# The order of SyncE's closing waits in a one-core SiLU MLP kernel, forward and backward

## Chip, cores and metric

The kernel runs on 1 core of one Trainium2 chip. The metric is device time in microseconds (us). A run is one execution; where several are given, the text says how many. The span in a profile goes from the first to the last instruction of the program; the device time is longer than the span by 1.8 us in most runs. Where the text below says what "the clock" tells, it means this measured device time; TensorE's own clock is named as such.

The change is a small one: its subject is the last microsecond of 320.

## The reference

```python
# x: [1, 2048, 640], w1: [640, 1536], w2: [1536, 640], grad_out: [1, 2048, 640], all bf16
h = jnp.einsum("bsd,df->bsf", x, w1)
h = jax.nn.silu(h)
out = jnp.einsum("bsf,fd->bsd", h, w2)
# returned: out and the gradients of x, w1 and w2 for grad_out (by jax.vjp)
```

## The kernel before

About 310 us of the kernel are one unbroken row of matmuls on TensorE. The head: 22 warm-up matmuls on a constant tile, then 20 transposes of the first rows of x, then the first real group.

```python
NWARM = 22
...
early = [nc.vector.memset(warm[:], 1.0)]
...
for i in range(NWARM):
    early.append(nc.tensor.matmul(wp[:, 0:P], lhsT=warm[:], rhs=warm[:], start=True, stop=True))
ident = cpool.tile([P, P], dt_in, name="ident")
make_identity(nc, ident[:])
...
early += [load_x_half(0), load_x_half(1), load_w1_rows(0, 1), load_w1_rows(1, KM)]
...
nc.tensor.transpose(tp[:, q, :], x_two[:, half, q, dt_ * P:(dt_ + 1) * P], ident[:])
```

The tail: the last tile of the gradient of w1 is computed in two parts, of 384 and 128 columns, and each part is stored as soon as it is evicted.

```python
for k, (lo, hi) in enumerate(((0, FC - P), (FC - P, FC))):
    ...                                     # 16 matmuls into gp[:, lo:hi]
    if k == 0:
        nc.scalar.activation(g1[:, lo:hi], gp[:, lo:hi], ACT.Copy)
    else:
        nc.vector.tensor_copy(out=g1[:, lo:hi], in_=gp[:, lo:hi])
    nc.sync.dma_start(out=gw1_v[:, dt_, fc * FC + lo:fc * FC + hi], in_=g1[:, lo:hi])
continue
```

The kernel's source has nothing after that. The framework adds a closing block: SyncE waits until eleven semaphores of DMAs and engines have their final values, then all engines meet in a barrier, the semaphores are cleared, and they meet once more. In the compiled program of before, SyncE's part of it reads as follows (a number is a semaphore: 101 and 104 to 110 count DMAs, 99, 100 and 102 count instructions of GpSimd, VectorE and ScalarE, TensorE's 103 is not waited for, 96 and 97 belong to the barrier; 101 is that of the 96 KB store, 104 that of the last one, of 32 KB):

```
EventSemaphore  wait 106, 105
EventSemaphore  wait 107, 104      <- the last store
EventSemaphore  wait 108, 101
EventSemaphore  wait 109, 100
EventSemaphore  wait 110, 102
Drain           wait 99
Drain           wait 97 == 0, then add 1 to 96     <- "reporting drain": SyncE is here
```

GpSimd waits until 96 has four such reports, and then releases the engines (in the trace of before its wait on 96 starts at 318.250 us, 33 ns after SyncE's reporting drain, and its update of 97 at 318.328). In the source this is one drain with a list of eleven waits, 99 first; in this program the compiler left the first of the list on the drain and put the others, two by two, into instructions ahead of it: five pairs and the drain in the trace.

Of the kernel before, what the change touches and what calls it, by code (L numbers as in the profile page):

```python
# [1 line left out]

# [12 lines left out]
def start_before_entry_wait(nc, names):  # L15




    def move(nc):  # L20
        blocks = nc.m.functions[0].blocks
        entry, home = blocks[0].instructions, blocks[1].instructions
        for engine in {i.engine for i in home if i.name in names}:
            mine = [i for i in home if i.engine == engine]
            last = max(k for k, i in enumerate(mine) if i.name in names)
            moved = mine[: last + 1]
            gate = next(
                k
                for k, i in enumerate(entry)
                if i.engine == engine and isinstance(i, mybir.InstEventSemaphore)  # L30
            )
            taken = {i.name for i in moved}
            for k in reversed(range(len(home))):
                if home[k].name in taken:
                    del home[k]
            for i in reversed(moved):
                entry.insert(gate, i)

    nc.at_finalize(move)

# [2 lines left out]
def kernel(  # L43
# [11 lines left out]
    nc = tc.nc  # L55
# [43 lines left out]
    def store_rows(c, pool):  # L99
        for scr, dst_v in ((oT_scr, out_v), (gxT_scr, gx_v)):  # L100
            o_sb = pool.tile([P, STC, D], dt_in, name="o_sb")
            nc.sync.dma_start_transpose(out=o_sb[:], in_=scr[:, c * SC:(c + 1) * SC])
            nc.sync.dma_start(out=dst_v[:, c * STC:(c + 1) * STC, :], in_=o_sb[:])
# [3 lines left out]
    def load_a_blk(fc, pool, tag=None):  # L107
        a_blk = pool.tile([P, ST, FC], dt_in, name="a_blk", tag=tag or "a_blk")
        nc.sync.dma_start_transpose(out=a_blk[:], in_=aT_scr[fc * FC:(fc + 1) * FC, :])
        a_blks.append(a_blk)  # L110

    with ExitStack() as mctx:
# [47 lines left out]
        early += [load_x_half(0), load_x_half(1), load_w1_rows(0, 1), load_w1_rows(1, KM)]  # L160
        load_w1_rows(KM, DT)
        start_before_entry_wait(nc, {i.ins.name for i in early})
        for fc in range(1, NFC):
            load_w1(fc * FC, (fc + 1) * FC)
# [147 lines left out]
    with ExitStack() as fctx:  # L312
        ab2pool = fctx.enter_context(tc.tile_pool(name="ab2pool", bufs=NFC - 1))
        gbpool = fctx.enter_context(tc.tile_pool(name="gbpool", bufs=NFC))
        fpool = fctx.enter_context(tc.tile_pool(name="fpool", bufs=NFC))
        s1pool = fctx.enter_context(tc.tile_pool(name="s1pool", bufs=3))

        for fc in range(1, NFC):
            load_a_blk(fc, ab2pool)
        gh_blks = []  # L320
        for fc in range(NFC):
            gh_blk = gbpool.tile([P, ST, FC], dt_in, name="gh_blk")
            nc.sync.dma_start_transpose(out=gh_blk[:], in_=ghT_scr[fc * FC:(fc + 1) * FC, :])
            gh_blks.append(gh_blk)

        store_rows(NCH - 1, s1pool)

        gw2_v = gw2.rearrange("(ft p) d -> p ft d", p=P)
        g2T_v = g2T_scr[:].rearrange("(dt p) f -> p dt f", p=P)
        k = 0  # L330
        for fc in range(NFC):
            a_blk = a_blks[fc]
            g2T = fpool.tile([P, DT, FC], dt_in, name="g2T")
            for dt_ in range(DT):
                gp = ps_h.tile([P, FC], FP32, name="hp")
                for st in range(ST):
                    nc.tensor.matmul(  # L337
                        gp[:],
                        lhsT=go_nat[:, st, dt_ * P:(dt_ + 1) * P],
                        rhs=a_blk[:, st, :],  # L340
                        start=(st == 0),
                        stop=(st == ST - 1),
                    )
                if k % 2 == 0:
                    nc.scalar.activation(g2T[:, dt_, :], gp[:], ACT.Copy)  # L345
                else:
                    nc.vector.tensor_copy(out=g2T[:, dt_, :], in_=gp[:])  # L347
                k += 1
            nc.sync.dma_start(out=g2T_v[:, :, fc * FC:(fc + 1) * FC], in_=g2T[:])

        def store_gw2(fc):
            g2 = fpool.tile([P, FB, D], dt_in, name="g2")
            nc.sync.dma_start_transpose(out=g2[:], in_=g2T_scr[:, fc * FC:(fc + 1) * FC])
            nc.sync.dma_start(out=gw2_v[:, fc * FB:(fc + 1) * FB, :], in_=g2[:])

        gw1_v = gw1.rearrange("(dt p) f -> p dt f", p=P)
        k = 0
        for fc in range(NFC):
            gh_blk = gh_blks[fc]
            for dt_ in range(DT):  # L360
                if dt_ == DT // 2:
                    store_gw2(fc)
                if fc == NFC - 1 and dt_ == DT - 1:
                    for k, (lo, hi) in enumerate(((0, FC - P), (FC - P, FC))):
                        gp = ps_h.tile([P, FC], FP32, name="hp")
                        for st in range(ST):
                            nc.tensor.matmul(  # L367
                                gp[:, lo:hi],
                                lhsT=x_nat[:, st, dt_ * P:(dt_ + 1) * P],
                                rhs=gh_blk[:, st, lo:hi],  # L370
                                start=(st == 0),
                                stop=(st == ST - 1),
                            )
                        g1 = s1pool.tile([P, FC], dt_in, name="g1")
                        if k == 0:
                            nc.scalar.activation(g1[:, lo:hi], gp[:, lo:hi], ACT.Copy)
                        else:
                            nc.vector.tensor_copy(out=g1[:, lo:hi], in_=gp[:, lo:hi])  # L378
                        nc.sync.dma_start(
                            out=gw1_v[:, dt_, fc * FC + lo:fc * FC + hi], in_=g1[:, lo:hi]  # L380
                        )
                    continue
                gp = ps_h.tile([P, FC], FP32, name="hp")
                for st in range(ST):
                    nc.tensor.matmul(  # L385
                        gp[:],
                        lhsT=x_nat[:, st, dt_ * P:(dt_ + 1) * P],
                        rhs=gh_blk[:, st, :],
                        start=(st == 0),
                        stop=(st == ST - 1),  # L390
                    )
                g1 = s1pool.tile([P, FC], dt_in, name="g1")
                if k % 2 == 0:
                    nc.scalar.activation(g1[:], gp[:], ACT.Copy)
                else:
                    nc.vector.tensor_copy(out=g1[:], in_=gp[:])  # L396
                k += 1
                nc.sync.dma_start(out=gw1_v[:, dt_, fc * FC:(fc + 1) * FC], in_=g1[:])
# [30 lines left out]
```

## Time and profile before

| | before |
|---|---|
| device time, median of the first 3 runs | 321.83 us (321.44 to 322.0) |
| device time of the profiled run | 320.68 us |
| span of the profiled run | 318.9 us |
| TensorE busy | 315.2 us, 99% |
| last matmul group's eviction starts | 316.10 us |
| last store (32 KB): issue, landing | 316.42 us, 317.90 us |
| SyncE's reporting drain starts | 318.217 us |
| landing of the last store to end of span | 1.011 us |

These are lines of the page of before: the span, the busy times of the engines, and the chain of work that ended last. In all such lines PE is TensorE with its matmuls, PEld its weight loads, DVE VectorE, ACT ScalarE, POOL GpSimd, SPq the queue of SyncE, and L424 line 424 of the kernel.

```profile
span 318.9 us, 3570 instructions
...
PE 315.2 (99%) x1498; PEld 145.4 (46%) x1498; DVE 102.2 (32%) x182; ACT 77.7 (24%) x142; POOL 0.7 (0%) x6
...
PE 98%; DMA 1%; DVE 1%; issue 0%; DVEq 0%; SPq 0%
```

TensorE is the whole chain, but for 1 to 2%. So what SyncE does in the middle holds up nothing that the chain shows; what it does when TensorE has finished should count fully, because then nobody else works. The next two lines are the DMA view of the stretch from 315 to 320 us of before: the two last stores, with size and microseconds from issue to landing.

```profile
out_dram<-g SPq DMA_DIRECT2D x1, 96.0 KB, 1.6
out_dram<-g SPq DMA_DIRECT2D x1, 32.0 KB, 1.5
```

The next line is from the view of waits of SyncE's queue (microseconds in total, times, longest), and the two after it are the instructions of the closing block on SyncE from 316.7 to 318.3 us (duration in ns: shortest, median, longest; then when the first and the last of them start).

```profile
SPq L424 <- DMA out_dram<-g: 1.1, 1, 1.1
```

```profile
L424 SPq EVENT_SEMAPHORE  x5: 28/28/1051, 316.8 to 318.1; - x5
L424 SPq DRAIN  x2: 7/10/13, 318.1 to 318.2; - x2
```

One of the five pairs of waits lasts 1.05 us, the other four 28 ns each. The trace has each of them as a record, so their starts can be listed (us from the span's start; this list is made from the records):

```
wait 106, 105        316.798   28 ns
wait 107, 104        316.867 1051 ns   ends 317.918; the last store landed at 317.896
wait 108, 101        317.957   28 ns
wait 109, 100        318.022   28 ns
wait 110, 102        318.083   28 ns
drain, wait 99       318.148   13 ns
reporting drain      318.217    7 ns
```

A wait that is met already still takes 61 to 69 ns from its start to the start of the next instruction. Four instructions stand between the wait that matters and the reporting drain.

### The profile page before, as it was taken

How to read it: one execution, taken by the hardware profiler on the slowest of the kernel's cores; microseconds unless marked ns; L12 is line 12 of the kernel's file. 1: busy time of each engine (PE TensorE's matmuls, PEld its weight loads, DVE VectorE, ACT ScalarE, POOL GpSimd, SP SyncE). 2: the span in 40 equal slices, each digit the busy share in tenths (PEclk: the TensorE clock that was granted, in tenths of full speed). 3: DMA queues.
4: the chain of work that ended last, by engine and by line, in shares of the span. 5: the costliest groups of instructions: out<-in, count | busy, mean ns of one | idle time of the engine just before them, and what ended most of it. 6: DMA issues, size and time to landing. Idle time of an engine off the chain costs nothing.

```text
span 318.9 us, 3570 instructions
## 1 busy us (share of the span) xinstructions
PE 315.2 (99%) x1498; PEld 145.4 (46%) x1498; DVE 102.2 (32%) x182; ACT 77.7 (24%) x142; POOL 0.7 (0%) x6
## 2 busy tenths in 40 slices
PE   9999999999999999999999999999999999999996
PEld 6444444444444444444444444444444444444443
DVE  2871641477410187700157741000001100001001
ACT  4951000644201354311065410111000001001100
POOL 0000000000000000000000000000000000000000
DMA  8999999998999866382643089719999998995011
GB/s 274 319 173 221 250 243 277 334 289 264 290 288 305 199 200 166 109 286 82 166 128 119 2 279 264 200 45 285 272 207 270 262 249 288 239 293 194 34 48 34
DMA packets 147311, 67.33 MB, mean 211 GB/s; under 512 B 112608, under 2 KB 147040, under 8 KB 147296
## 3 DMA queue, kind: packets, MB, share of 16 engines
q1 hardware_dynamic: 147296, 67.12, 81.5%
q8 instruction: 11, 0.18, 0.2%
q14 instruction: 4, 0.03, 0.0%
HBM read 9.83 MB, written 28.97 MB: 122 GB/s over the span
## 4 chain that ended last, share of the span: by engine, by line
PE 98%; DMA 1%; DVE 1%; issue 0%; DVEq 0%; SPq 0%
PE hp L249 32%; PE hp L186 16%; PE hp L337 16%; PE hp L233 16%; PE hp L385 15%; PE hp L367 1%; DMA x_two<-in_x_dram 1%; DVE xT L179 0%; PE tp L177 0%; DVE g L378 0%; DVEq L378 0%; SPq L413 0%
## 5 line engine op out<-in xcount | busy, mean ns | idle before, releaser
L186 PE MATMUL hp<-xT,w_nat 128*128 128x512 bf16 x240 | 56.9, 379 | 0.2 <-DVE xT L179 0.2
L233 PE MATMUL hp<-goT,w2T 128*128 128x512 bf16 x240 | 56.9, 379 | 0.0
L249 PE MATMUL hp<-aT,w_nat 128*128 128x512 bf16 x240 | 52.5, 379 | 0.0
L249 PE MATMUL hp<-ghT,w1T 128*128 128x512 bf16 x240 | 52.5, 379 | 0.0
L337 PE MATMUL hp<-a_blk,go_nat 128*128 128x512 bf16 x240 | 52.0, 379 | 0.0
L385 PE MATMUL hp<-gh_blk,x_nat 128*128 128x512 bf16 x224 | 48.5, 379 | 0.0
L257 ACT ACTIVATE oT<-hp 128x512 bf16<-128x512 f32 x24 | 14.3, 597 | 109.8 <-PE hp L249 109.8
L195 ACT ACTIVATE aT<-hp 128x512 bf16<-128x512 f32 x48 | 29.9, 625 | 32.8 <-PE hp L186 32.8
L186 PEld LDWEIGHTS <-w_nat 128*128 128x128 bf16 x240 | 23.5, 98 | 28.4 <-issue 0.4
L233 PEld LDWEIGHTS <-w2T 128*128 128x128 bf16 x240 | 23.5, 98 | 28.3
L337 PEld LDWEIGHTS <-go_nat 128*128 128x128 bf16 x240 | 23.5, 98 | 28.3
L249 PEld LDWEIGHTS <-w1T 128*128 128x128 bf16 x240 | 23.5, 98 | 28.3
L249 PEld LDWEIGHTS <-w_nat 128*128 128x128 bf16 x240 | 23.4, 98 | 28.3
L259 DVE CAST oT<-hp 128x512 bf16<-128x512 f32 x16 | 11.1, 692 | 77.0 <-PE hp L249 77.0
L240 DVE SCALAR_TENSOR_TENSOR ghT<-ghT,hp 128x512 bf16<-128x512 bf16 x48 | 32.5, 681 | 7.3 <-PE hp L233 7.3
L385 PEld LDWEIGHTS <-x_nat 128*128 128x128 bf16 x224 | 21.9, 98 | 26.4
L202 DVE SCALAR_TENSOR_TENSOR ghT<-aT,v 128x512 bf16<-128x512 bf16 x48 | 32.7, 686 | 0.5
L201 DVE TENSOR_SCALAR v<-t 128x512 bf16<-128x512 f32 x48 | 20.2, 425 | 30.1 <-ACT t L199 30.1
L199 ACT ACTIVATE t<-hp 128x512 f32<-128x512 f32 x48 | 29.8, 625 | 0.0
L396 DVE CAST g<-hp 128x512 bf16<-128x512 f32 x7 | 4.8, 691 | 47.1 <-PE hp L385 27.6
L347 DVE CAST g2T<-hp 128x512 bf16<-128x512 f32 x7 | 4.8, 692 | 46.1 <-PE hp L337 46.1
L345 ACT ACTIVATE g2T<-hp 128x512 bf16<-128x512 f32 x8 | 4.8, 597 | 47.0 <-PE hp L337 47.0
(20 smaller groups left out, 25.2 us busy)
## 6 DMA issues: line engine op xcount, KB each, us to landing
aT_scr<-aT SPq DMA_DIRECT2D x4, 1536.0 KB, 7.1
ghT_scr<-ghT SPq DMA_DIRECT2D x4, 1536.0 KB, 8.0
out_dram<-o_sb SPq DMA_DIRECT2D x8, 640.0 KB, 3.6
oT_scr<-oT SPq DMA_DIRECT2D x4, 640.0 KB, 3.6
go_nat<-in_grad_out_dram SPq DMA_DIRECT2D x4, 640.0 KB, 6.6
x_nat<-in_x_dram SPq DMA_DIRECT2D x4, 640.0 KB, 5.4
gxT_scr<-oT SPq DMA_DIRECT2D x4, 640.0 KB, 4.7
w_nat<-in_w_dram SPq DMA_DIRECT2D x1, 1920.0 KB, 13.7
```

Source lines behind the costliest of these rows:

```text
L186: nc.tensor.matmul(hp[:], lhsT=w1_nat[:, dt_, ft * P:(ft + 1) * P], rhs=xT[:, dt_, :], start=(dt_ == 0), stop=(dt_ == DT - 1),)
L195: nc.scalar.activation(aT[:, ft, :], hp[:], ACT.Silu)
L199: nc.scalar.activation(t[:], hp[:], ACT.Tanh, scale=0.5)
L201: nc.vector.tensor_scalar(out=v[:], in0=t[:], scalar1=-0.5, scalar2=0.5, op0=ALU.mult, op1=ALU.add)
L202: nc.vector.scalar_tensor_tensor(out=ghT[:, ft, :], in0=aT[:, ft, :], scalar=1.0, in1=v[:], op0=ALU.subtract, op1=ALU.mult)
L233: nc.tensor.matmul(gp[:], lhsT=w2T[:, dt_, ft * P:(ft + 1) * P], rhs=goT[:, dt_, :], start=(dt_ == 0), stop=(dt_ == DT - 1),)
L240: nc.vector.scalar_tensor_tensor(out=ghT[:, ft, :], in0=ghT[:, ft, :], scalar=1.0, in1=gp[:], op0=ALU.add, op1=ALU.mult)
L249: nc.tensor.matmul(op_[:], lhsT=w_all[:, ft, dt_ * P:(dt_ + 1) * P], rhs=rhs_all[:, ft, :], start=(ft == 0), stop=(ft == FT - 1),)
L257: nc.scalar.activation(oT[:, dt_, :], op_[:], ACT.Copy)
L259: nc.vector.tensor_copy(out=oT[:, dt_, :], in_=op_[:])
L337: nc.tensor.matmul(gp[:], lhsT=go_nat[:, st, dt_ * P:(dt_ + 1) * P], rhs=a_blk[:, st, :], start=(st == 0), stop=(st == ST - 1),)
L385: nc.tensor.matmul(gp[:], lhsT=x_nat[:, st, dt_ * P:(dt_ + 1) * P], rhs=gh_blk[:, st, :], start=(st == 0), stop=(st == ST - 1),)
```

## The change

The intent: all waits that are met early go ahead, and run while the last store is in flight; the wait for the last store comes last of all. A hook that runs when the program is complete puts its entry at the front of the list, since in before the first of the list is the one that stayed on the drain.

```diff
+import copy
...
+def wait_for_last_store_last(nc, name):
+    def move(nc):
+        blocks = nc.m.functions[0].blocks
+        store = next(i for b in blocks for i in b.instructions if i.name == name)
+        lanes = {u.id for u in store.sync_info.on_update}
+        end = blocks[-1].instructions
+        at = next(k for k, i in enumerate(end) if i.engine == mybir.EngineType.SP)
+        waits = list(end[at].sync_info.on_wait)
+        late = [w for w in waits if w.id in lanes]
+        assert len(late) == 1 and not end[at].sync_info.on_update
+        waits = late + [w for w in waits if w.id not in lanes]
+        end[at] = copy.replace(end[at], sync_info=mybir.SyncInfo(on_wait=waits, on_update=[]))
+
+    nc.at_finalize(move)
...
-                        nc.sync.dma_start(
+                        last_store = nc.sync.dma_start(
                             out=gw1_v[:, dt_, fc * FC + lo:fc * FC + hi], in_=g1[:, lo:hi]
                         )
+                    wait_for_last_store_last(nc, last_store.ins.name)
                     continue
```

## The prediction

> **What bounds the kernel.** The page gives PE 315.2 us busy of a 318.9 us span (99%), and the chain that ended last is 98% PE. The change touches none of that, only the tail. In the trace the last two stores (96 KB and 32 KB, line 379) are issued at 315.67 and 316.42 us; the 32 KB one lands at 317.90, 1.48 us after its issue. [...]1.48 us for 32 KB agrees with a latency, and the change doesn't shorten it.
>
> After the issue SyncE runs its closing sequence (line 424): five instructions that each wait for two semaphores, a drain with the eleventh wait, then the drain that reports to the closing barrier. The second pair holds the last store's semaphore: it starts at 316.87 and lasts 1.05 us (the view of waits: "SPq L424 <- DMA out_dram<-g: 1.1"), to 317.918, 22 ns after the landing. The others take 28 ns each, but behind the long one come three pairs and the drain, 61 to 66 ns from start to start: 317.957, 318.022, 318.083, drain 318.148 to 318.161, reporting drain 318.217. So 299 ns pass from the end of the long wait to the reporting drain, for semaphores that had their values long before.
>
> **What the change does.** The same eleven waits; the last store's moves to the front of the list. In the program of before, the first entry of that list (GpSimd's semaphore) stayed on the drain and the rest went into pairs ahead of it. So I expect the last store's wait alone on the drain, after the other ten in five pairs. Nothing is added or removed. [...]
>
> **Cost.** The five pairs then run while the last store is in flight. The latest semaphore among them is the 96 KB store's, landed at 317.29, in the second pair; three more pairs follow, so the drain starts to wait near 317.54, some 350 ns early. It ends about 22 ns after the landing, 317.92; the reporting drain follows 56 ns later, as it does now behind the drain: 317.975 instead of 318.217. Saving 299 - 56 = 243 ns, all on the critical path: the other engines' drains ended by 316.45, and GpSimd waits for four reports, of which SyncE's is last. The two barrier rounds behind it (0.68 us) are unchanged.
>
> Predicted: span 318.9 to 318.66; time 321.83 - 0.24 = 321.6 us, 0.08%, less than the 0.56 us spread of the three runs of before. Range 321.1 to 322.05. Chances: faster by over 2% 0.003, within 2% 0.994, slower by over 2% 0.003.
>
> **What would show it.** The pair with the 96 KB store lasts about 0.45 us, the other pairs 28 ns; the drain with the wait lasts about 0.38 us and ends within 30 ns of the last landing; from landing to the start of the reporting drain about 80 ns instead of 321; last landing to end of span about 0.77 us instead of 1.01. PE, DVE and ACT totals unchanged.
>
> **What would make it wrong.** The waits may be dealt out otherwise, with the last store's in an early pair (no gain, or up to 0.07 us lost). A waiting drain may release later than a semaphore instruction. The store's latency can vary between runs by as much as the gain. Run-to-run noise can hide or reverse it in the medians.

299 - 56 = 243 ns comes from the records of before's trace, and 321.83 - 0.24 = 321.6 us from its runs. That most of the last store's 1.48 us does not come from its size rests here on the store before it: with three times the bytes (96 KB) it took 1.62 us from issue to landing (315.67 to 317.29 us).

## The result, and the profile after

Throughout, a ratio is the mean time of one kernel's runs over the mean of the runs of before that are given with it, so it is not quite the ratio of the medians that stand beside it. Executions over 1.5% slower than the fastest of the same kernel are left out of the means.

| | before | after |
|---|---|---|
| median of 6 runs | 321.63 us (320.73 to 322.71) | 320.97 us (320.58 to 321.56) |
| ratio | | 0.9981, 95% interval 0.9958 to 1.0004 |
| span of the profiled run | 318.9 us | 319.4 us |
| landing of the last store to reporting drain | 0.321 us | 0.085 us |
| landing of the last store to end of span | 1.011 us | 0.775 us |

The median moved by 0.66 us where 0.24 was predicted, and the measured 320.97 us lies below the predicted range of 321.1 to 322.05. At the same time the profiled span of after is 0.5 us longer than that of before. Also, three of the six runs of before are those that the prediction started from (321.83, 322.0 and 321.44 us); the other three, 320.73, 320.97 and 322.71 us, have the median 320.97, the same as after. All this has to be put together.

The page of after, the same lines as of before:

```profile
span 319.4 us, 3541 instructions
...
PE 314.6 (98%) x1469; PEld 146.3 (46%) x1498; DVE 102.6 (32%) x182; ACT 77.9 (24%) x142; POOL 0.7 (0%) x6
...
PE 98%; DMA 1%; issue 1%; DVE 0%; DVEq 0%; SPq 0%
```

(29 records of matmuls are missing in this trace, 1469 of 1498; the weight loads are all there.) The last two stores, SyncE's wait, and its closing instructions from 317.4 to 318.8 us:

```profile
out_dram<-g SPq DMA_DIRECT2D x1, 96.0 KB, 1.6
out_dram<-g SPq DMA_DIRECT2D x1, 32.0 KB, 1.5
```

```profile
SPq L445 <- DMA out_dram<-g: 0.9, 2, 0.5
```

```profile
L445 SPq EVENT_SEMAPHORE  x5: 28/28/447, 317.6 to 318.2; - x5
L445 SPq DRAIN  x2: 7/10/13, 318.7 to 318.7; - x2
```

The stores take as long as before. The one wait of 1.1 us has become two of some 0.4 us: one for the 96 KB store (447 ns, in the second pair) and one for the last store. All five pairs start before 318.3 us, and both drains stand together at the end. From the records, again in us from the span's start:

```
wait 106, 105        317.553   28 ns
wait 107, 101        317.622  447 ns   the 96 KB store
wait 108, 100        318.108   28 ns
wait 109, 102        318.172   28 ns
wait 110, 99         318.233   28 ns
                                       the last store lands at 318.651
drain, wait 104      318.667   13 ns
reporting drain      318.736    7 ns
```

So the order is as intended, and the landing is followed by the report after 85 ns instead of 321. In the two traces the tail became 1.011 - 0.775 = 0.236 us shorter; 0.243 was predicted. The span became longer all the same, so something else in these two traces differs by 0.75 us. It is at the head. Timelines of TensorE's first 9 us, before and then after (start, duration, line, operation, count, idle time before it):

```profile
0.50 2.53 PE L125 MATMUL wp<-warm 128*128 128x128 bf16 x22 [0.50 <-DVE warm L121]
3.08 1.70 PE L177 MATMUL tp<-ident,x_two 128*128 128x128 bf16 x20
5.01 4.26 PE L186 MATMUL hp<-xT,w_nat 128*128 128x512 bf16 x19 [0.23 <-DVE xT L179]
```

```profile
0.50 2.53 PE L145 MATMUL wp<-warm 128*128 128x128 bf16 x22 [0.50 <-DVE warm L141]
3.19 2.31 PE L197 MATMUL tp<-ident,x_two 128*128 128x128 bf16 x20 [0.16 <-DMA x_two<-in_x_dram]
5.30 4.08 PE L206 MATMUL hp<-xT,w_nat 128*128 128x512 bf16 x15
```

The first real group starts at 5.01 us in one trace and at 5.30 in the other, and the 20 transposes took 1.70 and 2.31 us. The records give the spacing of TensorE's instructions. In before, the transposes follow each other every 107 ns at first and every 56 ns from 3.6 us on. In after they keep the 107 ns to the end, the first two matmuls of the first group take 419 and 427 ns to the next instead of 215, and the full rate comes only near 6.2 us. From the start of the first group to the last eviction before took 311.092 us and after 311.554; from there to the landing both took 1.794. That accounts for the difference of the spans: 0.293 later start, plus 0.462 in the row, minus 0.236 in the tail, is 0.519 (318.907 to 319.426).

The moment of this rate step is not the same from trace to trace: it came 3.1 us after the first matmul in before and 5.7 us after it in after, and the matmuls of both heads have gaps between them. All ten traces with 22 warm-up matmuls have it between these two; where the warm-up ran unbroken past the step it came 2.9 us (long_head, below) and 4.2 us (held_start_last) after the first matmul. What sets the moment, the traces do not show.

### The profile page after: what moved, and what is told of

Read it like the earlier page. It is cut to its first block, busy times and chain, and to the rows that moved or that the text cites. A ratio compares the mean times of both kernels' runs of the same rounds, so it can differ in the third digit from the quotient of the medians.

```text
span 319.4 us, 3541 instructions
## 1 busy us (share of the span) xinstructions
PE 314.6 (98%) x1469; PEld 146.3 (46%) x1498; DVE 102.6 (32%) x182; ACT 77.9 (24%) x142; POOL 0.7 (0%) x6
## 4 chain that ended last, share of the span: by engine, by line
PE 98%; DMA 1%; issue 1%; DVE 0%; DVEq 0%; SPq 0%
PE hp L269 32%; PE hp L206 16%; PE hp L357 16%; PE hp L253 16%; PE hp L406 15%; PE hp L387 1%; DMA x_two<-in_x_dram 1%; PE tp L197 1%; DVE g L398 0%; DVEq L398 0%; SPq L434 0%
```

## Theories

- Theory A: the change is worth the 0.24 us between landing and report; the rest of the 0.66 us is noise of the runs.
- Theory B (rival): the whole 0.66 us belongs to the change, by a way that the trace doesn't show.
- Theory C (rival): the closing waits don't count in the device time; all of the 0.66 us is noise.
- Theory D (rival, about the mechanism): it isn't the position that gained, but that a drain, not a semaphore instruction, now does the last wait.
- Theory E (formed on the way): what makes single runs differ by about 1 us is the head: the first loads of x and the moment of the rate step.

Diffs below are against the changed kernel, in the function `move`, if nothing else is said. Results were correct in all runs.

## The experiments

### Before and after once more

Both kernels were run again unchanged, each against before, in 5 rounds.

> The kernel before itself, once more, against itself: it measures the noise of the clock. Theory A (the change is worth the 0.24 us that the trace shows between the last landing and SyncE's report, and the rest of the measured 0.66 us is noise of the runs): ratio within 0.999 to 1.001, single runs spread over more than 0.6 us, and the profiled tail as before, about 321 ns from the last landing to the start of SyncE's reporting drain and about 1.01 us from landing to the end of the span. Theory B (the whole 0.66 us, ratio 0.998, belongs to the change): runs of one program agree much better than 0.66 us.

> The changed kernel once more. Theory A: ratio near 0.9993 (0.24 us of 321.6), with an interval that holds it; the tail in the trace as in the first run of the change, about 85 ns from landing to the reporting drain and 0.775 us from landing to end of span. Theory B: ratio again near 0.998 (0.6 us). Theory C (the closing waits don't count in the clocked time at all): ratio 1.000.

The kernel before against itself: 321.15 us (6 runs, 320.72 to 321.26) against 321.04 (11 runs, 320.75 to 322.01), ratio 0.9998 (0.9985 to 1.001). The changed kernel in the same rounds: 320.97 us (6 runs, 320.77 to 321.09), ratio 0.9993 (0.9979 to 1.0006). The tails in the traces: landing to reporting drain 311 and 86 ns, landing to end of span 1.000 and 0.775 us.

The changed kernel has its old median, 320.97; the one of before fell from 321.63 to 321.04 without an edit. So most of the 0.66 us was the draw of the first runs of before. The ratio is the one that theory A gives, but its interval holds 1 as well as 0.998: the clock, used like this, can't tell A, B and C apart. The tails repeat to within 11 ns.

### One step further: the reporting drain itself waits

> The last store's wait goes one step further: it changes places with the barrier-is-idle wait of the reporting drain, so that the drain that reports is itself the one that waits for the store. Theory A: the step from landing to the start of the reporting drain shrinks from 85 ns to about 16 ns (the 69 ns from start of one drain to start of the next are gone), landing to end of span from 0.775 to about 0.706 us, ratio near 0.9990 (0.31 us). Theories B and C say nothing more than for the changed kernel (0.998 or 1.000).

```diff
-        waits = late + [w for w in waits if w.id not in lanes]
-        end[at] = copy.replace(end[at], sync_info=mybir.SyncInfo(on_wait=waits, on_update=[]))
+        rest = [w for w in waits if w.id not in lanes]
+        report = next(k for k in range(at + 1, len(end)) if end[k].engine == mybir.EngineType.SP)
+        barrier = end[report].sync_info
...
+        end[at] = copy.replace(
+            end[at], sync_info=mybir.SyncInfo(on_wait=list(barrier.on_wait) + rest, on_update=[])
+        )
+        end[report] = copy.replace(
+            end[report], sync_info=mybir.SyncInfo(on_wait=late, on_update=list(barrier.on_update))
+        )
```

In the trace the reporting drain started 17 ns after the landing instead of 85, and landing to end of span was 0.706 us: both as expected. The clock says 321.27 us (6 runs, 320.49 to 321.8), ratio 1.0002 (0.9987 to 1.0017), so it shows nothing of it. The first group started at 5.62 us in this trace, the latest of the ten traces with 22 warm-up matmuls, and the heads of these ten differ by 0.61 us where the step is worth 0.07. So this version is the best tail of all in the trace, and not shown to be faster by the clock.

### Forty more waits behind the last store's

> The order of before, with 40 more pairs of waits that are met already put behind the last store's wait. Theory A (each such pair costs about 63 ns of the critical path): reporting drain about 321 + 40 x 63 = 2840 ns after the landing, time up by about 2.5 us, ratio near 1.008. Theory C: ratio 1.000. If pairs that are met already were overlapped in a long row, the slope would be smaller than 63 ns a pair.

```diff
-        waits = late + [w for w in waits if w.id not in lanes]
+        old_ones = [w for w in waits if w.id not in lanes and w.wait_value > 150]
+        n = 40
+        more = [old_ones[k % len(old_ones)] for k in range(n)]
+        waits = waits[:1] + more + waits[1:] + more
```

The last store's wait is in the second pair, as in before, and 40 pairs more come behind it. The closing instructions on SyncE from 318 to 321.3 us (with the long wait, which reaches into that stretch, and the barrier's):

```profile
L448 SPq EVENT_SEMAPHORE  x45: 17/28/1046, 317.3 to 321.2; - x45
L448 SPq DRAIN  x2: 7/7/7, 321.0 to 321.1; - x2
```

The reporting drain started 2.732 us after the landing. Against the 0.311 us of before's second trace that is (2732 - 311) / 40 = 60.5 ns for each pair. The time was 323.54 us (5 runs, 323.4 to 323.88) against 321.04, ratio 1.0076 (1.0062 to 1.009); 2.42 us of the trace would be 1.0075. So theory C falls: what SyncE does after the last landing is in the device time, one for one as far as the interval can tell (it stands for 2.0 to 2.9 us). A met wait costs 60 ns there, with 40 in a row as with three.

### Ten more waits, behind or ahead

> The order of before and ten more pairs of waits that are met already, all behind the last store's wait: the effect of the order is made large enough for the clock. Theory A: 10 x 60.4 ns (the slope of the run with 40 pairs) more than before: reporting drain 915 to 925 ns after the landing, time up by 0.60 us, ratio 1.0019. Theory D (what a SyncE wait costs does not depend on where it stands; the saving of the change comes from the drain instead of a semaphore instruction doing the last wait): the same here.

> The same twenty-one waits' worth of instructions, fifteen pairs and a drain, with the last store's wait alone on the drain and the wait for the 96 KB store in the last pair. Theory A: all fifteen pairs (15 x 62 = 930 ns) fit between the issue of the last store and its landing (1098 ns from the first pair's start in before), so the ten added pairs cost nothing: reporting drain 86 ns after the landing as in the changed kernel, ratio near 0.9993, and about 0.84 us (0.26%) below the run with ten pairs behind. Theory D: ratio above 1.001, the ten pairs cost 0.6 us here too.

```diff
-        waits = late + [w for w in waits if w.id not in lanes]
+        old_ones = [w for w in waits if w.id not in lanes and w.id != 101 and w.wait_value > 150]
+        more = [old_ones[k % len(old_ones)] for k in range(10)]
+        # ten_behind:
+        waits = waits[:1] + more + waits[1:] + more
+        # ten_ahead:
+        second = [w for w in waits if w.id == 101]
+        rest = [w for w in waits if w.id not in lanes and w.id != 101]
+        waits = late + second + more + rest + more
```

Behind, the reporting drain started 926 ns after the landing, ahead 75 ns: the same number of instructions, 0.851 us apart by order alone. SyncE's closing instructions with ten pairs ahead, from 316.5 to 318.3 us, are below: all fifteen pairs take 28 ns, none waits, and they have started by 318.0 us; only the drain waits.

```profile
L449 SPq EVENT_SEMAPHORE  x15: 28/28/28, 317.1 to 318.0; - x15
L449 SPq DRAIN  x2: 7/7/7, 318.2 to 318.3; - x2
```

The clock: behind 321.64 us (6 runs), ratio 1.0018 (1.0002 to 1.0033), as expected; ahead 321.47 us (6 runs, 320.68 to 321.87), ratio 1.0002 (0.9986 to 1.0018), expected was 0.9993, which the interval holds. Two of ahead's six runs, 321.87 and 321.67 us, have 2.9 and 2.6 us outside the span where 1.8 is usual; the mean of its six spans is 0.23 us below that of before's eleven, and this alone would be 0.9993. The traces decide here: landing to end of span 1.615 and 0.764 us. Theory D falls with them, and with the next two runs.

### The last store's wait in the last pair, and in the first

> The last store's wait in the fifth pair, with only the drain with GpSimd's wait behind it. Theory A (position alone counts, about 60 to 65 ns for each instruction behind): reporting drain 321 - 3 x 62 = about 135 ns after the landing (between 120 and 145). Theory D (the drain releases faster than a semaphore instruction and that is what the change gained): about 321 ns as before.

> The last store's wait in the first pair, one place earlier than in before. Theory A: one instruction more behind it, reporting drain about 321 + 62 = 383 ns after the landing (370 to 395). Theory D: about 321 ns.

```diff
-        waits = late + [w for w in waits if w.id not in lanes]
+        rest = [w for w in waits if w.id not in lanes]
+        waits = rest[:1] + late + rest[1:]      # last_pair
+        waits = rest[:6] + late + rest[6:]      # first_pair
```

One run each, for the trace (321.94 and 321.09 us; of a single run the state is unknown, so the times are not compared). The reporting drain started 129 ns after the landing with the wait in the last pair, and 413 ns with it in the first (expected 370 to 395). With the others this makes a row:

| position of the last store's wait | instructions behind it, up to the report | landing to reporting drain |
|---|---|---|
| first pair | 6 | 413 ns |
| second pair (before, two traces) | 5 | 321, 311 ns |
| last pair | 2 | 129 ns |
| drain (after, two traces) | 1 | 85, 86 ns |
| the reporting drain itself | 0 | 17 ns |

Theory D would have 321 ns everywhere but at the drain, so it falls: 129 ns are reached with a pair doing the last wait. Position decides, at 59 to 69 ns for each instruction behind. What the waiting instruction is adds a smaller term, and the expectation for the first pair missed it (413 ns measured, 370 to 395 expected). The records show the two forms. Where the last store is the second wait of a pair (before, and the last pair), the record of the pair contains the wait, ends 22 ns after the landing, and the next instruction starts some 60 ns after the landing. Where it is the first or only wait (the first pair, and the drain), the record begins 16 or 17 ns after the landing, and the next instruction starts 69 ns later, 85 or 86 after the landing. So the second form costs some 25 ns more. The drain itself comes in two kinds: 13 ns with 69 to the next instruction, or 7 ns with 59 (once 63). That is the difference between the 85 ns of after and the 75 of ten_ahead, and between the 321 and 311 of before's two traces; what decides between them is not known, so of a difference of 10 ns nothing is to be read here. This is the line of SyncE's closing pairs in the run with the first pair (from 317 to 318.8 us, one barrier instruction of 17 ns with them): the pair waited for the last store, and yet no record is longer than 28 ns.

```profile
L446 SPq EVENT_SEMAPHORE  x6: 17/28/28, 318.2 to 318.8; - x6
```

The prediction for the change had 22 + 56 = 78 ns for the drain where 16 + 69 = 85 came out.

### What makes the runs differ: a longer head

> The kernel before with 70 instead of 22 warm-up matmuls, so that the first transposes wait for the warm-up and no longer for the first loads of x, which is where the traces so far differ (the first matmul of the first group starts between 5.01 and 5.62 us, and two of ten traces ran the next few matmuls 0.4 us slower). Theory A (the spread of single runs comes from this head): the start of the first group later, at 6.5 to 8 us, time up by 1.5 to 2.5 us, and the spread of the six runs down to 0.4 us or less. If the spread stays near 1 us, it comes from elsewhere.

> The same 70 warm-up matmuls, with the last store's wait last as in the change. Theory A: 0.24 us (0.07%) below the run with the long head and the old order, now larger than the spread between medians if the head was the noise; landing to end of span 0.775 us. Theory B: 0.6 us below. Theory C: no difference.

```diff
-    NWARM = 22
+    NWARM = 70
```

Made on before (long_head) and on the changed kernel (long_head_last). The expectation failed. The times were 324.32 us (5 runs, 323.36 to 324.55) and, without one run of another kind (below), 323.26 to 324.62 us: 1.2 and 1.4 us of spread, as wide as ever, though the transposes no longer waited for the loads of x. In the trace of long_head, its fastest run, the rate step came near 3.4 us, after 28 of the 70 warm-up matmuls:

```profile
0.50 5.45 PE L125 MATMUL wp<-warm 128*128 128x128 bf16 x70 [0.50 <-DVE warm L121]
5.79 1.28 PE L177 MATMUL tp<-ident,x_two 128*128 128x128 bf16 x20
7.69 2.54 PE L186 MATMUL hp<-xT,w_nat 128*128 128x512 bf16 x11 [0.61 <-ACT xT L179]
```

Seventy matmuls at 107 ns would take 7.5 us, so this 5.45 us depends on when the step comes. By this estimate the step, with 70 of them on the path, sets the start more than it did before. That formed theory E.

### A head that neither loads nor the rate step can move

> The spread once more, as the run with 70 warm-up matmuls did not shrink it (323.36 to 324.55 us): the traces show that TensorE's first 128-column matmuls follow each other every 107 ns and then every 56 ns, and the moment of this step differs from trace to trace (about 3.6 us in before, after 5.2 us in the first trace of the change). With 70 warm-up matmuls on the path the step sets the start, so the spread must stay. Here the first transposes wait for a chain of fixed length on VectorE (eight memsets of 1024 columns[...]) while 120 warm-up matmuls run beside it, so that neither the loads nor the step set the start. Theory E (step and loads together make the spread): first group starts near 12 us, time up by about 6.5 us, spread of six runs 0.4 us or less except for executions with a longer time outside the span (0.7 us in a few so far). If the spread is near 1 us again, theory E falls too.

> The same held start with the last store's wait last. Theory A: 0.24 us (0.07%) below the run with the held start and the old order, in medians, if theory E holds and the spread has shrunk; landing to end of span 0.765 to 0.775 us instead of 1.00 to 1.01. Theory B: 0.6 us below. Theory C: no difference.

Measured in held_start_last: 0.91 us for a memset, one every 1.19 us, and a start at 11.61 us.

```diff
-    NWARM = 22
+    NWARM = 120
...
         make_identity(nc, ident[:])
+        spin = cpool.tile([P, 1024], FP32, name="spin")
+        for _ in range(8):
+            nc.vector.memset(spin[:], 0.0)
+        ident_late = cpool.tile([P, P], dt_in, name="ident_late")
+        nc.vector.tensor_copy(out=ident_late[:], in_=ident[:])
...
-    nc.tensor.transpose(tp[:, q, :], x_two[:, half, q, dt_ * P:(dt_ + 1) * P], ident[:])
+    nc.tensor.transpose(tp[:, q, :], x_two[:, half, q, dt_ * P:(dt_ + 1) * P], ident_late[:])
```

Made on before (held_start) and on the changed kernel (held_start_last). In the timeline of held_start_last, TensorE's head:

```profile
0.50 8.86 PE L145 MATMUL wp<-warm 128*128 128x128 bf16 x120 [0.50 <-DVE warm L141]
9.20 1.50 PE L202 MATMUL tp<-ident_late,x_two 128*128 128x128 bf16 x20
11.61 2.75 PE L211 MATMUL hp<-xT,w_nat 128*128 128x512 bf16 x11 [0.91 <-DVE xT L204]
```

The head is held, but not in the way that was intended. The intent was that the transposes wait for `ident_late`, which is made behind the eight memsets. In this trace VectorE made it at 7.81 us, before the last two memsets, and the transposes started at 9.20 us, right behind the last warm-up matmul. What holds the start is VectorE itself: its memsets take 0.91 us each, one every 1.19 us, and only after the last of them does it copy the transposes out, which the first real group waits for. The last links of the chain of this trace up to 13 us (start, duration, what):

```profile
9.36 0.91 DVE spin L151
10.27 1.29 DVE xT L204 x4
11.57 0.04 issue
11.61 0.59 PE hp L211 x2
```

The single runs:

| | runs, us | mean |
|---|---|---|
| held start, order of before | 327.27, 327.26, 327.28, 327.29 | 327.275 |
| held start, last store's wait last | 327.04, 327.06, 327.04, 327.03, 327.07 | 327.048 |

With the head held, the spread falls from about 1 us to 0.04 us, and the two kernels are apart by 327.275 - 327.048 = 0.227 us, and the gap between the two groups of runs (327.07 to 327.26) is more than four times as wide as either group. The order of the waits is the only difference of the two programs. So theory A stands on the clock too: the change is worth 0.23 us, and not 0.66 (B) nor 0 (C). The traces say 0.225 to 0.236 (landing to end of span 1.000 or 1.011 us against 0.775).

The held start itself is no improvement, it costs 6 us (ratios 1.0187 and 1.0180 to before). Theory E stands as far as this: loads and rate step together make the spread of the spans; their shares were not separated. The spread of the times has a second source, which theory E leaves out: the time outside the span. Of the 85 executions with 22 warm-up matmuls whose span is on record, 73 have 1.7 to 2.0 us outside it and 12 have 2.1 to 2.9. Its cause is not known. The nine normal runs with the held head all have 1.7 to 1.8 us; whether that is the held head or luck is open. For the spans, theory E agrees with the ten traces with 22 warm-up matmuls: the row from the first real matmul to the last eviction took 311.091 to 311.096 us in eight of them, and 311.50 and 311.55 in the two in which the rate step came after the row had begun.

One execution of held_start, the profiled one, took 1216.25 us, and one of long_head_last, again the profiled one, 1205.59 us. They count as slow and are left out above; the tail of held_start (1.000 us) is read from that slow trace. Two lines of its page, the span and the group of the first real matmuls (busy us, mean ns of one, idle time before), say what it was:

```profile
span 1214.5 us, 3741 instructions
...
L191 PE MATMUL hp<-xT,w_nat 128*128 128x512 bf16 x232 | 201.6, 1105 | 4.3 <-issue 4.3
```

A matmul has 1105 ns instead of 379, from the beginning to the end of the execution (in the chain of long_head_last 240 matmuls of 512 columns take 197.06 us, 821 ns each, where the records of before have 215 or 216 ns from one to the next); VectorE and ScalarE were busy only 5% and 2% longer than in held_start_last, and the granted clock reads 1.0. Both kernels have more warm-up matmuls than the others (120 and 70); whether that is the cause is open, as all their other executions were normal.

## Why the prediction was right or wrong

Right, point by point:

- What moves where: the last store's wait alone on the drain, the ten others in five pairs, with the 96 KB store's in the second pair. The trace shows just that order.
- The pair with the 96 KB store lasts 447 ns (0.45 predicted), the others 28 ns.
- From the landing to the start of the reporting drain 85 ns (about 80 predicted, from 321).
- Last landing to the end of the span 0.775 us (0.77 predicted). The saving is 0.236 us (0.243 predicted), and 0.227 us on the clock when the head is held.
- All of it on the critical path: shown by the 40 added waits, 2.42 us in the trace and 1.0076 on the clock.

Wrong:

- The step that failed is the base of the sum, "time 321.83 - 0.24 = 321.6 us", with its "Range 321.1 to 322.05". The 321.83 was a median of three runs. The same program has medians of 321.04 (11 runs), 321.30 (11), 321.17 (11) and 321.16 (9) in the later sessions. From 321.16 the same sum gives 320.92; measured were 320.97 and 320.97. The term of the change was right to 0.02 us and the base was 0.5 to 0.8 us too high. The warning was at hand: the profiled run of before took 320.68 us, 0.76 below the lowest of the three timed runs and below the range that was then given. The range was drawn around the three and not around all four. What made these three slow stays open: neither their spans nor their chip are on record (the later sessions ran on four different chips).
- "span 318.9 to 318.66": the profiled span of after was 319.4. The tail's saving was there, but the head of that execution was 0.75 us slower (0.29 us until the first real group, 0.46 in the row behind it until the full rate came). The prediction named noise in the medians and in the store's latency, and not the head. The store's latency was steady: 1.469 to 1.478 us in all fourteen traces.
- "the drain with the wait lasting about 0.38 us": its record is 13 ns long and starts 16 ns after the landing. So the wait is not in the record. The other half of the sentence, that it ends within 30 ns of the landing, held (29 ns).
- "PE, DVE and ACT totals unchanged" holds for DVE and ACT within 0.4 us; the total of PE read 0.6 us less, with 29 records missing, so nothing is to be read from it.

## What to carry to other kernels

When the last transfer of a program has landed, count the instructions that still stand between it and the end: each wait there cost some 60 ns here even if it was met long ago, and putting the latest wait last hid all the others at no cost. A gain below the spread of single runs is read in the trace from an anchor close to it (here the landing), not from spans or medians; if the clock must show it, find what moves the runs and hold it, as the held head brought the spread from 1 us to 0.04; and look in the trace whether it is held by what was meant to hold it. And base a forecast on all runs there are, the profiled one too: three runs of a program that varies by 1 us are no base for a range of 1 us.
